# A streamed x + alpha * fx: the first x load in two parts, the first sum in place

## The chip, the core and the metric

The kernel runs on one core of a Trainium2 chip. The metric is the device time of one execution in microseconds (us), as a median of runs. VectorE (DVE) does the arithmetic, SyncE (SP) issues nearly all transfers, and sixteen DMA engines carry them between HBM, the chip's main memory, and SBUF, the core's on-chip memory of 128 partitions.

## The reference

```python
B, S, D = 512, 32, 640
x, fx: (B, S, D) bfloat16;  alpha: (1,) bfloat16

def reference(x, fx, alpha):
    return x + alpha * fx
```

Each of the three large arrays has 512 * 32 * 640 = 10,485,760 elements, 20.97 MB. Two are read and one is written, 62.92 MB in all.

## The kernel before

Each array is seen as 128 rows (one for each partition) of 81,920 elements, and is worked through in K = 5 chunks of CHUNK = 16,384 columns. One chunk of one array is 128 rows of 32 KB, 4 MB, and is moved by one transfer. The row of a partition is 160 KB in HBM, so a chunk's row is one contiguous piece of it.

At the start `alpha_to_lanes` (line 16) brings the scalar to all partitions: a tiny load issued by ScalarE, a matmul with a row of ones, and a copy into `a_f`. After that, one chunk is: load x (line 65), load fx (line 69), one VectorE instruction over the whole chunk (line 76, `scalar_tensor_tensor`: fx times `a_f` plus x), and a store (line 87). The last chunk is summed and stored in two halves.

SBUF holds four slots for x tiles (tags x0 to x3) and two for fx tiles. The list `slot_x` says which slot a chunk's x is loaded into, `slot_o` which slot its sum goes to. Chunk 0 is loaded into slot 0 and summed into slot 3. Chunks 1, 2, 3 and 4 are summed in place, in slots 1, 2, 0 and 3.

All loads and stores are issued by SP on one queue, in the order in which lines 92 to 112 are written: the schedule is written out by hand. SP waits, with everything behind it, where a transfer needs a slot that is still in use or a sum that isn't done. The x and fx loads of chunks 0 and 1 and the x load of chunk 2 need no wait. The fx load of chunk 2 goes into the slot of chunk 0's fx, and waits for the first sum. The x load of chunk 3 goes into slot 0, which the first sum reads. The x load of chunk 4 goes into slot 3, from which the store of chunk 0 reads.

Of the kernel before, what the change touches and what calls it, by code (L numbers as in the profile page):

```python
# [1 line left out]

# [4 lines left out]

ACT = mybir.ActivationFunctionType
ALU = mybir.AluOpType
F32 = mybir.dt.float32  # L10
BF16 = mybir.dt.bfloat16

CHUNK = 16384


def alpha_to_lanes(nc, consts, psum, alpha, eng):

    P = nc.NUM_PARTITIONS
    a_1 = consts.tile([1, 1], alpha.dtype, name="a_1")
    eng.dma_start(out=a_1[:], in_=alpha[None, :])  # L20
    ones = consts.tile([1, P], alpha.dtype, name="ones")
    nc.vector.memset(ones[:], 1.0)  # L22
    a_ps = psum.tile([P, 1], F32, name="a_ps")
    nc.tensor.matmul(a_ps[:], ones[:], a_1[:], start=True, stop=True)  # L24
    a_f = consts.tile([P, 1], F32, name="a_f")
    nc.vector.tensor_copy(out=a_f[:], in_=a_ps[:])  # L26
    return a_f


@with_exitstack  # L30
def kernel(
    ctx: ExitStack,
    tc: tile.TileContext,
    x: bass.AP,
    fx: bass.AP,
    alpha: bass.AP,
    out: bass.AP,
):
    nc = tc.nc
    P = nc.NUM_PARTITIONS  # L40
    xv = x.flatten_outer_dims().rearrange("(p n) d -> p (n d)", p=P)
    fxv = fx.flatten_outer_dims().rearrange("(p n) d -> p (n d)", p=P)
    ov = out.flatten_outer_dims().rearrange("(p n) d -> p (n d)", p=P)
    F = xv.shape[1]
    K = F // CHUNK
    assert K * CHUNK == F and K == 5

    consts = ctx.enter_context(tc.tile_pool(name="consts", bufs=1))
    psum = ctx.enter_context(tc.tile_pool(name="psum", bufs=1, space=bass.MemoryType.PSUM))
    xs = ctx.enter_context(tc.tile_pool(name="xs", bufs=1))  # L50
    fs = ctx.enter_context(tc.tile_pool(name="fs", bufs=2))
    ctx.enter_context(tc.manual_schedule())

    a_f = alpha_to_lanes(nc, consts, psum, alpha, nc.scalar)

    slot_x = [0, 1, 2, 0, 3]
    slot_o = [3, 1, 2, 0, 3]
    xt, ot, ft = {}, {}, {}

    def x_slot(i):  # L60
        return xs.tile([P, CHUNK], x.dtype, tag=f"x{i}", name="x_t")

    def load_x(k):
        xt[k] = x_slot(slot_x[k])
        nc.sync.dma_start(out=xt[k][:], in_=xv[:, bass.ts(k, CHUNK)])  # L65

    def load_f(k):
        ft[k] = fs.tile([P, CHUNK], fx.dtype, tag="f", name="f_t")
        nc.sync.dma_start(out=ft[k][:], in_=fxv[:, bass.ts(k, CHUNK)])

    def compute(k, parts=1):
        n = CHUNK // parts
        ot[k] = xt[k] if slot_o[k] == slot_x[k] else x_slot(slot_o[k])
        for j in range(parts):
            s = bass.ts(j, n)
            nc.vector.scalar_tensor_tensor(  # L76
                out=ot[k][:, s],
                in0=ft[k][:, s],
                scalar=a_f[:],
                in1=xt[k][:, s],  # L80
                op0=ALU.mult,
                op1=ALU.add,
            )

    def store(k, j=0, parts=1):
        n = CHUNK // parts
        nc.sync.dma_start(
            out=ov[:, k * CHUNK + j * n : k * CHUNK + (j + 1) * n],
            in_=ot[k][:, bass.ts(j, n)],
        )  # L90

    load_x(0)
    load_f(0)
    load_x(1)
    load_f(1)
    load_x(2)
    compute(0)
    load_f(2)
    store(0)
    load_x(3)  # L100
    compute(1)
    load_f(3)
    store(1)
    load_x(4)
    compute(2)
    load_f(4)
    store(2)
    compute(3)
    store(3)
    compute(4, 2)  # L110
    store(4, 0, 2)
    store(4, 1, 2)


# [1 line left out]
_INS = ['x', 'fx', 'alpha']  # L116
_OUTS = [((512, 32, 640), 'bfloat16')]


# [23 lines left out]
```

## Time and profile before

| | us |
|---|---|
| median of 3 runs (153.01 to 153.89) | 153.03 |
| the profiled execution | 153.03 |
| span of the profiled execution (first to last instruction) | 151.3 |
| VectorE busy | 86.9 |
| one sum of 128 x 16384 (x4) | 17.28 |
| one sum of 128 x 8192 (x2) | 8.75 |
| VectorE idle ahead of line 76, ended by the landing of an fx load | 50.0 |
| median time from issue to landing: x load, fx load, full store | 34.8, 32.3, 36.8 |

The span is what the profiler saw between the first and the last instruction; the execution's own time is 1.73 us longer. The rate over the span is 416 GB/s. "Issue to landing" contains the time that a transfer stands behind others that were issued before it, which is most of it here.

### The profile page before, as it was taken

The numbers are of one execution on the slowest core, as the hardware profiler recorded it, in microseconds if no ns is written. First come the engines' busy times: TensorE is split into PE (matmuls) and PEld (weight loads), VectorE is DVE, ScalarE is ACT, GpSimd is POOL, SyncE is SP. The second block draws the span as 40 slices with busy tenths as digits, with TensorE's granted clock in tenths as the row PEclk, the third lists the DMA queues.
The fourth block names the chain that finished last, engine by engine and source line by source line (L and its number), as shares of the span: only waits on it lengthen the run. The fifth ranks groups of instructions, "written<-read, shape, count | busy, mean of one in ns | idle before, by whom it ended". The sixth has DMA issues, their size and how long they took to land.

```text
span 151.3 us, 85 instructions
## 1 busy us (share of the span) xinstructions
PE 0.2 (0%) x1; PEld 0.1 (0%) x1; DVE 86.9 (57%) x8; POOL 0.2 (0%) x4
## 2 busy tenths in 40 slices
PE   0000000000000000000000000000000000000000
PEld 0000000000000000000000000000000000000000
DVE  0000009999679997499991006999900089997000
POOL 0000000000000000000000000000000000000000
DMA  6999999999999999999999999999999999998993
GB/s 182 442 451 442 416 425 416 425 451 442 451 442 416 425 416 399 381 433 425 425 433 425 425 407 459 459 433 416 416 433 433 416 442 468 425 433 373 442 429 169
DMA packets 2306, 62.92 MB, mean 416 GB/s; under 512 B 258, under 2 KB 258, under 8 KB 258
## 3 DMA queue, kind: packets, MB, share of 16 engines
q1 hardware_dynamic: 2304, 62.92, 97.7%
q10 hardware_dynamic: 2, 0.00, 0.0%
HBM read 41.94 MB, written 20.97 MB: 416 GB/s over the span
## 4 chain that ended last, share of the span: by engine, by line
DMA 56%; DVE 29%; DVEq 6%; SPq 0%; issue 0%
DMA f_t<-in_fx_dram 56%; DVE x_t L76 29%; DVEq L138 6%; SPq L65 0%; DVEq L76 0%
## 5 line engine op out<-in xcount | busy, mean ns | idle before, releaser
L76 DVE SCALAR_TENSOR_TENSOR x_t<-f_t,a_f,x_t 128x16384 bf16<-128x16384 bf16 (+1 forms) x6 | 86.5, 14438 | 50.0 <-DMA f_t<-in_fx_dram 50.0
L26 DVE COPY a_f<-a_ps 128x1 f32<-128x1 f32 x1 | 0.2, 159 | 1.1 <-PE a_ps L24 1.1
L22 DVE MEMSET ones<- 1x128 bf16 x1 | 0.2, 165 | 0.8 <-PEq L127 0.8
L24 PE MATMUL a_ps<-a,ones 1*128 1x1 bf16 x1 | 0.2, 158 | 1.9 <-DMA a<-in_alpha_dram 1.9
L127 POOL MEMSET const-bfloat16-1.0<- 128x1 bf16 x1 | 0.1, 101 | 0.0
L127 POOL MEMSET const-uint8-127<- 128x1 uint8 x1 | 0.1, 101 | 0.0
L24 PEld LDWEIGHTS <-ones 1*128 1x128 bf16 x1 | 0.1, 98 | 1.0 <-DVE ones L22 1.0
L127 POOL MEMSET const-float32-0.0<- 128x1 f32 x1 | 0.1, 98 | 0.2 <-issue 0.2
L127 POOL MEMSET const-float32-1.0<- 128x1 f32 x1 | 0.1, 98 | 0.0
## 6 DMA issues: line engine op xcount, KB each, us to landing
x_t<-in_x_dram SPq DMA_DIRECT2D x5, 4096.0 KB, 34.8
f_t<-in_fx_dram SPq DMA_DIRECT2D x5, 4096.0 KB, 32.3
out_dram<-x_t SPq DMA_DIRECT2D x4, 4096.0 KB, 36.8
out_dram<-x_t SPq DMA_DIRECT2D x2, 2048.0 KB, 15.4
a<-in_alpha_dram ACTq DMA_DIRECT2D x1, 0.0 KB
```

The source lines that it names most:

```text
L22: nc.vector.memset(ones[:], 1.0)
L24: nc.tensor.matmul(a_ps[:], ones[:], a_1[:], start=True, stop=True)
L26: nc.vector.tensor_copy(out=a_f[:], in_=a_ps[:])
L76: nc.vector.scalar_tensor_tensor(out=ot[k][:, s], in0=ft[k][:, s], scalar=a_f[:], in1=xt[k][:, s], op0=ALU.mult, op1=ALU.add,)
L127: nc = _bacc.Bacc("TRN2", target_bir_lowering=False, num_devices=1)
L138: with _tile.TileContext(nc) as tc:
```

## The change

The x tiles come from one tag with four buffers in rotation: chunk k goes to slot k mod 4, and chunk 4 to slot 0 again. Every sum is written in place, and the store reads the x tile. The load of chunk 0's x is issued as two transfers, partitions 0 to 15 and then 16 to 127; the other loads and all stores are single transfers as before. The order of loads, sums and stores is the same but for the one extra issue.

```diff
-    xs = ctx.enter_context(tc.tile_pool(name="xs", bufs=1))
+    xs = ctx.enter_context(tc.tile_pool(name="xs", bufs=4))
...
-    slot_x = [0, 1, 2, 0, 3]
-    slot_o = [3, 1, 2, 0, 3]
-    xt, ot, ft = {}, {}, {}
-
-    def x_slot(i):
-        return xs.tile([P, CHUNK], x.dtype, tag=f"x{i}", name="x_t")
+    xt, ft = {}, {}

     def load_x(k):
-        xt[k] = x_slot(slot_x[k])
-        nc.sync.dma_start(out=xt[k][:], in_=xv[:, bass.ts(k, CHUNK)])
+        xt[k] = xs.tile([P, CHUNK], x.dtype, tag="x", name="x_t")
+        for a, b in [(0, 16), (16, P)] if k == 0 else [(0, P)]:
+            nc.sync.dma_start(out=xt[k][a:b, :], in_=xv[a:b, bass.ts(k, CHUNK)])
...
     def compute(k, parts=1):
         n = CHUNK // parts
-        ot[k] = xt[k] if slot_o[k] == slot_x[k] else x_slot(slot_o[k])
         for j in range(parts):
             s = bass.ts(j, n)
             nc.vector.scalar_tensor_tensor(
-                out=ot[k][:, s],
+                out=xt[k][:, s],
...
-            in_=ot[k][:, bass.ts(j, n)],
+            in_=xt[k][:, bass.ts(j, n)],
```

## The prediction

> **What bounds the kernel now.** I read the page first, then the stretches of the DMA engines, then the order of issues in the timeline and SP's waits. The strips over 40 slices and the DMA queue come first:
>
> ```profile
> DVE  0000009999679997499991006999900089997000
> DMA  6999999999999999999999999999999999998993
> DMA packets 2306, 62.92 MB, mean 416 GB/s; under 512 B 258, under 2 KB 258, under 8 KB 258
> ...
> q1 hardware_dynamic: 2304, 62.92, 97.7%
> ```
>
> The reader is to see that VectorE has long empty stretches while the DMA strip is full from the second slice on. The chain of waits says the same in another way (DMA 56%, VectorE's line 76 29%): its VectorE pieces are links of the chain, but transfers run beneath them all the time, since the strip has no gap. So the sixteen DMA engines set the time, and only what changes their work, their pace, their start or their end can move it.
>
> The packets tell how a transfer is cut. 2304 on q1 is 16 transfers (ten loads, six stores) of 128 rows, 2048 in all, plus 256 short ones, which is 16 per transfer: one closing packet on each engine. A full load is therefore 8 rows of 32 KB on each engine, and the whole run is 62.92 MB / 16 / 32,768 B = 120 row times on each.
>
> The start of the first load, in half microseconds (the columns end with the DMA share and GB/s; a packet is counted whole where it starts, so a share can pass 1):
>
> ```profile
> 1.50:2.00 0.50, 0.07 (x1) 0.00 (x0) 0.00 (x0) 0.00 (x0) 1.00 3.11 786
> 2.00:2.50 0.50, 0.09 (x1) 0.00 (x0) 0.16 (x1) 0.00 (x0) 1.00 0.60 197
> 2.50:3.00 0.50, 0.00 (x0) 0.00 (x0) 0.00 (x0) 0.00 (x0) 1.00 0.15 66
> 3.00:3.50 0.50, 0.00 (x0) 0.00 (x0) 0.00 (x0) 0.00 (x0) 1.00 0.00 0
> 3.50:4.00 0.50, 0.00 (x0) 0.00 (x0) 0.00 (x0) 0.00 (x0) 1.00 1.88 786
> ...
> 5.00:5.50 0.50, 0.00 (x0) 0.00 (x0) 0.00 (x0) 0.00 (x0) 1.00 1.52 655
> ```
>
> 786 GB/s for 0.5 us is 12 rows; 197 is three, 66 is one. So twelve engines begin before 2.0, three by 2.5, one after 2.5. The first twelve rows last 3.11 x 0.5 x 16 / 12 = 2.07 us each. In the last line shown ten rows last 1.52 x 0.5 x 16 / 10 = 1.22 us. I use 1.21 us for a settled row (the 1 us stretches further on give 1.21 to 1.22).
>
> In stretches of 10 us:
>
> ```profile
> 2.00:12.00 10.00, 0.09 (x1) 0.00 (x0) 0.16 (x1) 0.00 (x0) 1.00 0.89 380
> 12.00:22.00 10.00, 0.00 (x0) 0.00 (x0) 0.00 (x0) 0.00 (x0) 1.00 1.02 439
> ...
> 52.00:62.00 10.00, 0.00 (x0) 0.00 (x0) 7.71 (x1) 0.00 (x0) 1.00 1.04 406
> ```
>
> At 1.21 us a row sixteen engines move 433 GB/s, and most of the run is at 420 to 440. Rows alone take 120 x 1.21 = 145.2 us. With 1.7 us ahead of the first packet that is 146.9 of a span of 151.3. The other 4.4 us are the end (hardly anything starts after 149), the slow first rows (2.07 - 1.21 = 0.86) and places such as 52 to 62, where loads and the first store meet (406 against 433 GB/s, 0.6 us). The profiled execution took 153.03 us, 1.73 outside its span, and the median of the three runs is 153.03 too; what I add to the span I add to 153.03.
>
> **The change part by part.** *The slot of the first sum.* Before, chunk 0 is summed from slot 0 into slot 3; after, in place. Nothing is computed differently. The four full sums take 17.28 to 17.29 us, though the first has its own output and the other three run in place: 0.
>
> *The waits that move.* Before, the x load of chunk 3 goes into slot 0 and waits for the first sum; after, into the untouched slot 3 without a wait. But SP issues in order:
>
> ```profile
> 40.35 0.33 SPq L69 DMA_DIRECT2D f_t<-in_fx_dram  x1
> 40.72 0.43 SPq L87 DMA_DIRECT2D out_dram<-x_t  x1
> 41.26 0.38 SPq L65 DMA_DIRECT2D x_t<-in_x_dram  x1
> ...
> 72.70 0.33 SPq L65 DMA_DIRECT2D x_t<-in_x_dram  x1
> ```
>
> The store of chunk 0, and the fx load ahead of it, still wait for the same sum, which ends at 40.33, so the x load leaves at 41.26 as before: 0. The x load of chunk 4 waits for the landing of the first store in both kernels (slot 3 before, slot 0 after), and leaves at 72.70. Behind it stand the fx load of chunk 4 and the stores. The engines then hold the x and fx loads of chunk 3 and the store of chunk 1, three transfers of 9.7 us, so the cover is some 29 us: 0. The first store gains a wait for the two parts of x, which the first sum has already waited for: 0.
>
> *One more issue on SP.* The first load becomes two instructions. An issue and its gap take 0.43 to 0.64 us here (starts 0.73, 1.16, 1.64, 2.11, 2.75), so the four loads behind leave some 0.5 us later. They queue behind 9.7 us of rows and are covered. The second part itself leaves at about 1.16 and can reach the engines at about 2.1 (first packets come 0.6 us after their issue ends), while the first rows hold their engines until 3.5. The cover is 1.4 us; without it the price would be one issue, 0.5 us.
>
> *Sixteen more closing packets.* What is left of the 4.4 us after the slow first rows and the end (about 1.3) is 2.2 us over 16 transfers, slow stretches included, so a boundary costs at most 0.14 us. I take 0.1.
>
> *The pace of the first 0.5 MB.* This is the term that decides, and the trace of before shows no transfer that covers part of the partitions. The bytes on each engine are unchanged if both parts go over all sixteen engines: one row each, then seven. If a row keeps its 1.21 us whatever partitions the other rows go to, nothing is added, and an earlier first row could take something off. At most the latest engine's lag is saved: it begins after 2.5 where the first begin after 1.7, about 0.9 us. That is the lower end, -0.9. For the upper end I let a transfer's pace follow the partitions it spans. Sixteen of 128 partitions would then take as long as a full load of the same row length, 8 x 1.21 = 9.7 us in place of 1.21: +8.5. The nearest row for rows that get in each other's way are the twelve first ones, 2.07 against 1.21, a factor of 1.7, where the upper end is a factor of 8. Neither end has a row of its own, so I take the middle of 0 and 8.5, +4.2, and keep both.
>
> [...]
>
> Would it come back later? The engines are busy 97.7% of the span and have the same 120 row times to do, so what a lane loses at the start it ends late by, and the latest lane sets the end. VectorE's sums, which have 38.0 and 12.0 us of idle time, only move along. Sum: 0 + 0 + 0 + 0.1 + 4.2, so 153.0 + 4.3 = 157.3 us. The stagger could spread over the 112 rows as well, so this case runs from 154.6 to 161.5.
>
> **The rivals.** *Even spreading* (not slower). The first sixteen rows go one to each engine and keep near 1.21 us. This happens at the start of the first load, and decides if those rows take less than about 2.1 us each, as the first rows do today. For it: all 16 closing packets per transfer show sixteen engines at work, and a settled row's time hardly varies. Price: from +0.1 down to -0.9, 152.1 to 153.1 us, within 1%. [...]
>
> *A better rhythm.* The early stagger keeps the lanes from meeting where loads and stores mix. Besides the 0.9 at the start it would win the 0.6 us of the stretch from 52 to 62 and something of its neighbours: 151.4 us or less. Against it: that needs almost all that is not rows, start or end.
>
> *Rows on few engines.* If the sixteen rows went to one engine, 16 x 1.21 - 1.21 = 18.2 us would be added to it: 171.2. The 16 closing packets of each transfer speak against it.
>
> **How the numbers follow.** A measurement of this kernel can tell about 1% from no change, 1.5 us. Crowded rows 0.60, of which 0.05 cost less than 1.5 us; even spreading 0.30; a better rhythm 0.05; few engines 0.05. So faster 0.05, same 0.30 + 0.05, slower 0.55 + 0.05. The range goes from 152.3, inside even spreading, to 161.5, the upper end of crowding. It leaves out the better rhythm, the few engines and a little of even spreading.
>
> **What would show it.** Crowding: in the first 10 us the share stays near 1 while GB/s falls well under 380, the first fx load lands later than 22.9 us, by 3 to 8 us, and every later piece of the chain shifts by as much, with sums of 17.29 us as before. Even spreading: the fx load lands at 22 to 23.5. The slot's part is right if the x loads of chunks 3 and 4 still follow right behind the first store's issue and its landing. I am wrong if the time falls, or if the shift of the first fx load does not reach the end.

## The result and the profile after

| | before | after |
|---|---|---|
| median, us (4 runs each) | 153.02 (152.48 to 153.89) | 162.26 (162.13 to 162.7) |
| ratio, 95% interval | | 1.0603, 1.0550 to 1.0657 |
| profiled execution, its span | 153.03, 151.3 | 162.22, 160.4 |
| bytes, packets on q1 | 62.92 MB, 2304 | 62.92 MB, 2320 |
| VectorE busy | 86.9 | 86.9 |

The kernel is 9.24 us slower. It moves the same bytes and VectorE does the same work. The strips of the changed kernel's page, in 40 slices of 4.0 us:

```profile
DVE  0000000099994999949999000999930049998000
...
DMA  9799999999999999999999999999999999999991
GB/s 131 139 261 286 253 351 441 449 417 425 449 433 400 457 441 400 441 466 400 433 449 425 425 449 417 408 449 441 417 417 474 392 417 466 417 425 425 400 445 53
DMA packets 2322, 62.92 MB, mean 392 GB/s; under 512 B 274, under 2 KB 274, under 8 KB 274
...
q1 hardware_dynamic: 2320, 62.92, 97.1%
```

The reader is to compare the second and third lines. The engines count as busy from the first slice on (the 7 in the second comes of counting a packet whole where it starts), but for the first five slices they move 131 to 286 GB/s, and from the seventh on some 430. A share of busy time alone would have shown nothing: the share of q1, SP's queue, is 97.1%, it was 97.7%. The 16 extra packets are the closing ones of one more transfer, as many as every other transfer has and as there are engines. And in the changed kernel sixteen rows begin before 2.5 us (786 and 262 GB/s in the half microseconds from 1.5 and 2.0, twelve rows and four) and none from there to 4.0. So I take both parts to go over all sixteen; the trace doesn't name a packet's engine.

The same in stretches of 10 us, and closer at the start (the last two columns are DMA share and GB/s):

```profile
2.00:12.00 10.00, 0.09 (x1) 0.00 (x0) 0.16 (x1) 0.00 (x0) 1.00 0.80 174
12.00:22.00 10.00, 0.00 (x0) 0.00 (x0) 0.00 (x0) 0.00 (x0) 1.00 1.00 272
22.00:32.00 10.00, 0.00 (x0) 0.00 (x0) 0.00 (x0) 0.00 (x0) 1.00 1.02 439
...
1.50:2.00 0.50, 0.07 (x1) 0.00 (x0) 0.00 (x0) 0.00 (x0) 1.00 5.51 786
...
12.00:16.00 4.00, 0.00 (x0) 0.00 (x0) 0.00 (x0) 0.00 (x0) 1.00 1.04 279
16.00:20.00 4.00, 0.00 (x0) 0.00 (x0) 0.00 (x0) 0.00 (x0) 1.00 1.04 262
```

Before, these first two stretches had 380 and 439 GB/s. The first twelve rows now last 5.51 x 0.5 x 16 / 12 = 3.67 us each, where they lasted 2.07. These belong to the 16-partition part. From 12 to 20, well inside the 112-partition part, a row lasts 1.04 x 4 x 16 / 34 = 1.96 us and then 1.04 x 4 x 16 / 32 = 2.08 us, where a settled row of before lasts 1.21. So both parts are slow, and the pace is back once whole 128-partition transfers are under way.

How the delay goes on, in the timeline of the changed kernel:

```profile
32.31 17.29 DVE L70 SCALAR_TENSOR_TENSOR x_t<-f_t,a_f,x_t 128x16384 bf16<-128x16384 bf16 x1 [30.02 <-DMA f_t<-in_fx_dram]
49.62 0.33 SPq L64 DMA_DIRECT2D f_t<-in_fx_dram  x1
50.06 0.37 SPq L81 DMA_DIRECT2D out_dram<-x_t  x1
50.47 0.43 SPq L60 DMA_DIRECT2D x_t<-in_x_dram  x1
...
80.73 0.33 SPq L60 DMA_DIRECT2D x_t<-in_x_dram  x1
...
130.55 17.41 DVE L70 SCALAR_TENSOR_TENSOR x_t<-f_t,a_f,x_t 128x8192 bf16<-128x8192 bf16 x2 [12.83 <-DMA f_t<-in_fx_dram]
```

The same two sums before:

```profile
23.04 17.29 DVE L76 SCALAR_TENSOR_TENSOR x_t<-f_t,a_f,x_t 128x16384 bf16<-128x16384 bf16 x1 [20.76 <-DMA f_t<-in_fx_dram]
...
121.40 17.41 DVE L76 SCALAR_TENSOR_TENSOR x_t<-f_t,a_f,x_t 128x8192 bf16<-128x8192 bf16 x2 [11.98 <-DMA f_t<-in_fx_dram]
```

The first sum starts 9.27 us later than before (32.31 against 23.04), the last pair of sums 9.15 later (130.55 against 121.40), and the span is 9.1 longer. What was lost by the time the first fx tile landed stays lost to the end; nothing is added later and nothing is recovered. The in-place first sum still takes 17.29 us.

### The profile page after: what moved, and what is told of

Its sections match the earlier page's. It is cut to its first block, busy times and chain, and to the rows that moved or that the text cites. A ratio compares the mean times of both kernels' runs of the same rounds, so it can differ in the third digit from the quotient of the medians.

```text
span 160.4 us, 88 instructions
## 1 busy us (share of the span) xinstructions
PE 0.2 (0%) x1; PEld 0.1 (0%) x1; DVE 86.9 (54%) x8; POOL 0.2 (0%) x4
## 2 busy tenths in 40 slices
DMA packets 2322, 62.92 MB, mean 392 GB/s; under 512 B 274, under 2 KB 274, under 8 KB 274
## 3 DMA queue, kind: packets, MB, share of 16 engines
q1 hardware_dynamic: 2320, 62.92, 97.1%
## 4 chain that ended last, share of the span: by engine, by line
DMA 59%; DVE 27%; DVEq 5%; SPq 0%; issue 0%
DMA f_t<-in_fx_dram 59%; DVE x_t L70 27%; DVEq L132 5%; SPq L60 0%; DVEq L70 0%
```

## The experiments

Theories after the result. *Groups*: rows that are under way at the same time slow each other if their partitions belong to one group, as if they shared a path, and a part of the tile brings more such rows together than the whole. This is an assumption of the author; no run shows a path, or which partitions make up a group. *Splitting as such*: two transfers for one tile, one more issue and wait. *Short transfers*: a transfer with few rows is slow wherever it goes. *Source*: neighbouring rows in memory are slow to read. *Slots*: the other half of the change.

**The slots alone.** The changed kernel with the split taken out:

```diff
-        for a, b in [(0, 16), (16, P)] if k == 0 else [(0, P)]:
-            nc.sync.dma_start(out=xt[k][a:b, :], in_=xv[a:b, bass.ts(k, CHUNK)])
+        nc.sync.dma_start(out=xt[k][:], in_=xv[:, bass.ts(k, CHUNK)])
```

> The change without its split: the x tiles in four rotating slots and the first sum in place, the first x load one transfer of 128 partitions again. If the split makes the whole difference, the time is that of before, 153.0 us (within 0.5), and the first sum starts at 23.0 us. If the slots have a part in it (the in-place first sum, or the x load of chunk 4 that now waits on slot 0), the time stands between 153.0 and 162.3, and the sums or the two x loads behind the first store move.

Measured: 152.76 us against 152.74 of before, ratio 1.0003 (0.9973 to 1.0033). The first sum starts at 22.67. The slots cost nothing and win nothing that can be measured (0.3%, 0.5 us), so the 9.24 us are the split's. This kernel is the base of the runs with extra loads below and of the last run.

**The same split, by columns.**

```diff
-        for a, b in [(0, 16), (16, P)] if k == 0 else [(0, P)]:
-            nc.sync.dma_start(out=xt[k][a:b, :], in_=xv[a:b, bass.ts(k, CHUNK)])
+        for a, b in [(0, 2048), (2048, CHUNK)] if k == 0 else [(0, CHUNK)]:
+            nc.sync.dma_start(out=xt[k][:, a:b], in_=xv[:, k * CHUNK + a : k * CHUNK + b])
```

> The first x load in two transfers of the same 0.5 MB and 3.5 MB, but cut by columns: 2048 columns of all 128 partitions, then 14336. Theory crowding (few partitions at a time are slow): 153 us, at most 0.5 from before, since both parts span all partitions. Rival splitting as such (two transfers for one tile, one more issue, one more wait): near 162 us as the changed kernel.

Measured: 152.44 us, ratio 0.9993 (0.9969 to 1.0017). Two transfers, the same two sizes, one more issue and one more wait cost nothing here when both span 128 partitions (152.74 before). Splitting as such falls.

**Sixteen rows to adjacent partitions, and the same rows spread.** Both kernels have four extra loads behind the first fx load, with the same source rows. They differ in the partitions alone. The comments stand here only; `load_x(3)`, not shown, later loads into this same tile and takes no new one:

```diff
     load_x(0)
     load_f(0)
+    xt[3] = xs.tile([P, CHUNK], x.dtype, tag="x", name="x_t")
+    for i in range(4):
+        nc.sync.dma_start(out=xt[3][16 * i : 16 * i + 16, :],   # adjacent
+                          in_=xv[16 * i : 16 * i + 16, bass.ts(3, CHUNK)])
...
+        nc.sync.dma_start(out=xt[3][32 + i : 96 : 4, :],        # spread
+                          in_=xv[16 * i : 16 * i + 16, bass.ts(3, CHUNK)])
```

> The kernel of the first experiment with four more loads behind the first fx load: each brings 16 rows of 32 KB into 16 adjacent partitions (0 to 15, 16 to 31, 32 to 47, 48 to 63) of the slot that chunk 3's x overwrites later; output unchanged. Each engine gets four more rows. Evenly they cost 4 x 1.21 = 4.85 us: about 157.9. Theory crowding by adjacent partitions: clearly more; the changed kernel's 112-row part ran at about 272 GB/s in place of 433, which would make 7.7 us here, 160.7, and the upper end of the prediction (pace follows the partitions spanned) makes 4 x 9.7 = 38.8, 191.8. [...]

> The same four extra loads with the same 16 source rows each, but into partitions 32 to 95 in steps of four (32, 36, ... 92, then 33, 37, ... and so on). Theory crowding by adjacent partitions: the rows no longer meet, 4 x 1.21 = 4.85 us, about 157.9, and rows of 1.21 us. Rival short transfers (any transfer of 16 rows is slow, wherever it goes) and rival source (rows that are neighbours in memory are slow to read): the same time as the run with adjacent partitions.

Measured: adjacent 170.61 us, ratio 1.1171 (1.1123 to 1.1218); spread 157.94, ratio 1.0341 (1.0301 to 1.0381); before 152.74 beside both. That is 17.9 us against 5.2 for the same bytes from the same source rows in transfers of the same form. The stretch in which the extra loads run, adjacent partitions first:

```profile
24.00:30.00 6.00, 0.00 (x0) 0.00 (x0) 5.20 (x1) 0.00 (x0) 1.00 1.08 131
```

and in the spread kernel, where four row times behind the first two loads are over much sooner:

```profile
21.60:25.80 4.20, 0.00 (x0) 0.00 (x0) 3.16 (x1) 0.00 (x0) 1.00 1.13 484
```

131 GB/s for 6 us is 24 rows, so a row to adjacent partitions lasts 1.08 x 6 x 16 / 24 = 4.32 us. Spread, 484 GB/s for 4.2 us is 62 of the 64 extra rows, at 1.13 x 4.2 x 16 / 62 = 1.22 us. In both the DMA share is above 1. Short transfers fall: sixteen rows went at the settled pace, 1.22 against 1.21 us. Each of these two kernels ran twice, as did the next two.

**Half as spread.** The same step of four, but within partitions 0 to 63:

```diff
-        nc.sync.dma_start(out=xt[3][32 + i : 96 : 4, :],
+        nc.sync.dma_start(out=xt[3][i : 64 : 4, :],
```

> As the run with four extra loads of 16 rows, into partitions 0, 4, ... 60 and then 1, 5, ... 61 and so on: a step of four as in the run that cost 5.2 us, but within partitions 0 to 63. [...] Rival adjacency (only neighbouring partitions get in each other's way): as the spread run, 5.2 us, 157.9. Rival shape: no matter.

Measured: 163.17 us against 153.14 of before, 10.0 us more, ratio 1.0645 (1.0533 to 1.0757).

```profile
24.00:30.00 6.00, 0.00 (x0) 0.00 (x0) 6.00 (x1) 0.00 (x0) 1.00 1.06 218
```

Forty rows last 1.06 x 6 x 16 / 40 = 2.54 us each, twice a settled row. No two partitions of one transfer are neighbours here, so adjacency falls in its plain form: rows to partitions that are not neighbours are slow as well. The three runs with the same source rows form a scale of 1.22, 2.54 and 4.32 us by their partitions. Whether single partitions between 0 and 63 get in each other's way, or that half as a whole has half the pace, no run here tells apart cleanly.

**Source rows apart.** The kernel with adjacent partitions, its rows read eight apart:

```diff
-                          in_=xv[16 * i : 16 * i + 16, bass.ts(3, CHUNK)])
+                          in_=xv[i : 128 : 8, bass.ts(3, CHUNK)])
```

> As the run with four extra loads into 16 adjacent partitions, which cost 17.9 us, but the 16 source rows of each are eight rows apart in memory (1.25 MB) in place of neighbours; what lands there is overwritten by chunk 3's x as before. Theory groups: the source doesn't matter, 17.9 us again, 170.6. Rival source (neighbouring rows are slow to read): near 5 us, 158.

Measured: 171.74 us, 18.6 more than before, ratio 1.1205 (1.1111 to 1.1298), where neighbouring source rows had cost 17.9. Source falls.

**Cut in halves.**

```diff
-        for a, b in [(0, 16), (16, P)] if k == 0 else [(0, P)]:
+        for a, b in [(0, 64), (64, P)] if k == 0 else [(0, P)]:
```

> The changed kernel with the first x load cut at partition 64: 0 to 63, then 64 to 127. [...] Rival even: 153.

Measured: 163.79 us, 10.65 more than before, ratio 1.0690 (1.0627 to 1.0752). These two halves go at half the pace, one after the other, through the whole load (68 rows at 1.07 x 10 x 16 / 68 = 2.52 us in the first stretch, 63 at 0.99 x 10 x 16 / 63 = 2.51 us in the second):

```profile
2.00:12.00 10.00, 0.07 (x1) 0.00 (x0) 0.16 (x1) 0.00 (x0) 1.00 1.07 223
12.00:22.00 10.00, 0.00 (x0) 0.00 (x0) 0.00 (x0) 0.00 (x0) 1.00 0.99 206
```

A pace in proportion to the partitions spanned, which is how the prediction had put its upper end, would give half the pace too, 8 x 1.21 = 9.7 us more, so this run doesn't tell it from groups. The next one does.

**Cut in 64 other rows and twice 32.**

```diff
-        for a, b in [(0, 16), (16, P)] if k == 0 else [(0, P)]:
+        for a, b in [(32, 96), (0, 32), (96, P)] if k == 0 else [(0, P)]:
```

> The first x load in three parts: partitions 32 to 95, then 0 to 31, then 96 to 127. [...] Rival pace by partitions spanned: half pace for 64 and a quarter for 32, 4.85 + 2 x 7.3 = 19.4 us more, 172. Rival even: 153.

Measured: 157.60 us, 4.46 more than before, ratio 1.0315 (1.0228 to 1.0403), where proportion said 19.4.

```profile
4.00:7.00 3.00, 0.00 (x0) 0.00 (x0) 0.00 (x0) 0.00 (x0) 1.00 1.20 513
...
8.00:16.00 8.00, 0.00 (x0) 0.00 (x0) 0.00 (x0) 0.00 (x0) 1.00 1.00 213
```

In the first line 47 rows last 1.20 x 3 x 16 / 47 = 1.23 us, in the second 52 rows last 1.00 x 8 x 16 / 52 = 2.46 us: the rows of partitions 32 to 95 go at full pace, those of the two parts of 32 at half pace. So 64 partitions are slow or not according to which they are: 2.52 us a row for 0 to 63, 1.23 for 32 to 95. It also fits that each engine takes a run of adjacent rows, four in a part of 64: the rows under way together would then lie four partitions apart, as in the runs with a step of four, which had 2.54 us over 0 to 60 and 1.22 over 32 to 92. The trace doesn't name a packet's engine, so that is inferred.

**The second part by itself.** One extra load of 112 rows to partitions 16 to 127:

```diff
+    xt[3] = xs.tile([P, CHUNK], x.dtype, tag="x", name="x_t")
+    for i in range(1):
+        nc.sync.dma_start(out=xt[3][16 : P, :], in_=xv[16:P, bass.ts(3, CHUNK)])
```

> The kernel of the first experiment with one more load behind the first fx load: 112 rows into partitions 16 to 127 of the slot that chunk 3's x overwrites later; output unchanged. Seven rows on each engine, evenly 7 x 1.21 = 8.5 us: 161.5. [...] From the changed kernel: it lost 9.2 us in all; 16 adjacent rows cost 17.9 / 4 = 4.5 us in place of 1.2 in the run with four such loads, so 3.3 of the 9.2 are the first part's and 5.9 the second's, which gives 8.5 + 5.9 = 14.4 here, 167.4. If the 112-row part costs nothing beyond its bytes, the first part's cost must have another source.

Measured: 167.72 us against 152.99, 14.7 more, ratio 1.0952 (1.0876 to 1.1027). That is 6.2 us beyond the 8.5 of its bytes. In its midst:

```profile
24.00:34.00 10.00, 0.00 (x0) 0.00 (x0) 10.00 (x1) 0.00 (x0) 1.00 1.00 259
```

79 rows at 1.00 x 10 x 16 / 79 = 2.03 us, as in the changed kernel. The expectation had 14.4 us, worked out from the changed kernel. Why rows to these 112 partitions take 2.03 us is not shown: as no run tells which partitions make up a group, groups give no number for them.

**A store cut in halves.**

```diff
-        nc.sync.dma_start(
-            out=ov[:, k * CHUNK + j * n : k * CHUNK + (j + 1) * n],
-            in_=xt[k][:, bass.ts(j, n)],
-        )
+        for a, b in [(0, 64), (64, P)] if k == 0 else [(0, P)]:
+            nc.sync.dma_start(
+                out=ov[a:b, k * CHUNK + j * n : k * CHUNK + (j + 1) * n],
+                in_=xt[k][a:b, bass.ts(j, n)],
+            )
```

> No load is split; the store of chunk 0 is issued as two transfers, partitions 0 to 63 and 64 to 127, the cut that cost 10.7 us on the first x load. Theory groups holding for what is read from the partitions as for what is written: 9.7 to 10.7 us more, 163 to 164. If only writes into the partitions share a path: 153. In between if loads that run beside the store fill the time.

Measured: 161.20 us against 152.99, 8.2 more, ratio 1.0524 (1.0463 to 1.0584). In the stretch of that store:

```profile
62.00:80.00 18.00, 0.00 (x0) 0.00 (x0) 17.28 (x1) 0.00 (x0) 1.00 1.00 253
```

A store that is cut by partitions is slow too, if by 8.2 us where the load lost 10.65. Six loads of eight row times lie ahead of it (6 x 8 x 1.21 = 58 us, behind 1.7 us at the start and slower first rows), so by estimate it begins at about 61 us. Its start by that estimate, and a stretch further on:

```profile
61.00:63.40 2.40, 0.00 (x0) 0.00 (x0) 1.18 (x1) 0.00 (x0) 1.00 0.99 423
...
70.00:76.00 6.00, 0.00 (x0) 0.00 (x0) 6.00 (x1) 0.00 (x0) 1.00 0.93 191
```

From 70 to 76, 35 rows last 0.93 x 6 x 16 / 35 = 2.55 us, as in the load cut at 64 (2.52), so reading from the partitions was no milder there. The first 31 rows, two on each engine if they spread evenly, last 0.99 x 2.4 x 16 / 31 = 1.23 us; two rows that escape the half pace save some 2 x 1.3 us, which is about what the store lost less. That they are the store's, and why they escape, is not shown. No run cuts this store by columns; the last store of the kernel of before goes in two halves by columns, and the engines move 421 GB/s there (142 to 149 us).

## Why the prediction was wrong

The direction was right, and so was crowding as the cause, in that the same split costs nothing on all 128 partitions (152.44 us). Where it acts and its size were not: 157.3 was forecast, with a range to 161.5, and 162.26 came.

- *Bound.* Right. The DMA engines set the time, VectorE's sums and idle time only moved along, and the loss of the first load reached the end in full (9.27 us at the first sum, 9.1 in the span).
- *The slot and the moved waits at nothing.* Right: 152.76 against 152.74 without the split. The x load of chunk 3 still leaves behind the first store's issue (50.47 after 50.06), that of chunk 4 at 80.73.
- *One more issue at nothing, sixteen more closing packets at 0.1.* Right within what can be measured: the split by columns has both and takes 152.44 against 152.74.
- *The pace of the first 0.5 MB.* This step failed. The middle of 0 and 8.5 was taken, +4.2, a choice between two ends and no measurement. The 16-partition part by itself costs 17.9 / 4 - 1.2 = 3.3 us, which the step would have covered. But it was the only part that had a price. Of the other 112 rows the prediction said that "the stagger could spread over the 112 rows as well", and gave that no number. They cost 14.7 - 8.5 = 6.2 us. Together that is 9.5 us, against 9.24 measured in the changed kernel, but in part this agreement is luck: the first rows are slow without a split too, and in the changed kernel the first twelve last only 1.6 us longer than before (3.67 against 2.07), so there the 112 rows bear still more of the 9.24. The term should have been made of two: one row per engine at 3.6 times its time (4.32 against 1.21), and seven rows at 1.7 times (2.03).
- *The upper end* was no bound for the same reason. It let the sixteen rows go at an eighth of the pace and the 112 at full pace. By its own rule the 112 rows would have taken 9.7 us as well, 1.2 more than their 8.5, and the whole would have been 153.0 + 9.7 + 0.1 = 162.8, near the measured time by luck: 8.5 and 1.2 stand where the runs with extra loads have 3.3 and 6.2. A pace in proportion to the partitions spanned is also the wrong rule: 64 rows go at 1.23 us or at 2.52 by which rows they are.
- *Even spreading* and *a better rhythm* fall. *Rows on few engines* falls by the sixteen rows that begin before 2.5 us, and by the 16 more closing packets. The saving of up to 0.9 us on a late first row came in no measurable size, not even in the split by columns, which has a small first part on all partitions.
- *What would show it.* The GB/s under 380 was as foretold (174); the share, foretold near 1, read 0.80 in the first ten us and 1.00 in the next; the first fx load landed 9.3 us later, beyond the 3 to 8 given.

No version here beats both kernels by more than can be measured.

## What to carry to other kernels

When a transfer between memory and the core's partitions is split, cut it by columns and keep all 128 partitions in each part: here the same cut cost nothing by columns and 9.24 us by partitions. If it must be cut by partitions, measure every part, the large remainder too: in the runs with extra loads the 16 partitions cost 3.3 us beyond their bytes and the other 112 cost 6.2, and as a part of the first load 64 partitions took 1.23 us a row (32 to 95) or 2.52 (0 to 63). And read GB/s beside the DMA share: a slow row counts as busy time, so the share of the whole run stayed at 97% although the pace in the second slice of 4.0 us was 139 GB/s, a third of the later 430.

## What the runs showed of the hardware

Sixteen 32 KB rows at a time took 1.22 us each when spread over partitions 32 to 92 in steps of four, 2.54 us over 0 to 60 in the same steps, and 4.32 us on sixteen neighbours. The rows of a load to the 64 partitions from 32 to 95 took 1.23 us each, a settled row's time (1.21), and those to the 64 from 0 to 63 took 2.52, twice that. A 112-partition load was no cheaper than a 128-partition one: 14.7 us against 8 x 1.21 = 9.7, for an eighth fewer bytes. The cut at 64 cost 10.65 us on a 4 MB load, about its whole time of 9.7 us again.
